# An fp32 Fourier-mixing and feed-forward kernel: moving columns read by turns from the two halves of a row, sums with the residual read in steps of four

## The chip, the cores and the metric

The kernel runs on one core of a Trainium2 chip. The metric is the device time of one execution in microseconds (us), the median of three runs; beside the runs there is one execution taken with the hardware profiler, which has its own time and the trace. The engines are called TensorE (PE, with its weight loads PEld), VectorE (DVE), ScalarE (ACT), GpSimd (POOL) and SyncE (SP).

## The reference

All arrays are fp32; S = 2048 positions, D = 512 features, F = 1792 hidden features.

```python
def reference(A_x, A_dft_seq_re, A_dft_seq_im, A_dft_hid_re, A_dft_hid_im, B_x, B_w1, B_w2):
    def _A_ref(x, dft_seq_re, dft_seq_im, dft_hid_re, dft_hid_im):
        a = jnp.einsum("bsd,ed->bse", x, dft_hid_re)
        b = jnp.einsum("bsd,ed->bse", x, dft_hid_im)
        y = jnp.einsum("ts,bse->bte", dft_seq_re, a) - jnp.einsum("ts,bse->bte", dft_seq_im, b)
        return y
    def _B_ref(x, w1, w2):
        h = jnp.einsum("bsd,df->bsf", x, w1)
        h = _silu(h)
        out = jnp.einsum("bsf,fd->bsd", h, w2)
        return out
    x = A_x
    h = x + _A_ref(_layernorm(x, axis=-1), A_dft_seq_re, A_dft_seq_im, A_dft_hid_re, A_dft_hid_im)
    h2 = h + _B_ref(_layernorm(h, axis=-1), B_w1, B_w2)
    return h2
```

So there are two residual sums: `h = x + A(...)` and `h2 = h + B(...)`.

## The kernel before

Everything is held transposed: features on the 128 partitions, positions in the free dimension, 512 positions to a row. A matmul takes a weight tile of 128x128 as the stationary operand and a row of 512 columns as the moving one, and adds into a bank of the accumulator memory with 512 fp32 columns. The columns of the moving row and of the bank stand for positions, in the same order.

To reach fp32 accuracy every operand is split into two parts, a rounded high part and the remainder (`rounded`, L263: ScalarE copies at L266, VectorE subtracts at L270 or L272). A product is then three matmuls, issued by the helper `three` (L314 to L318): high x high, high x remainder, remainder x high. In the first steps of the kernel the same three are issued in another order, grouped over four outputs (L513, L515, L517, in `plain`). The large products are done as two-by-two block products with seven instead of eight multiplications, which is why there are numbered products 1 to 7, sums of blocks before them and sums of results behind them.

The stages, in the order in which TensorE runs them:

- `plain(0, 0)`, `fast(1, 0)`: the position transform (cosine, then sine matrix) of the normalised x, for half q = 0 of the positions. Stationary: x. Moving: rows of the position matrices, from memory. Results c and m, copied out in the order in which they lie.
- `mix_fast(0)`: the feature transform. Stationary: the feature matrices. Moving: the results of the stage before. The banks are copied out by `copy_out` (L848) or added to the transposed x by `residual` (L868, by way of the `add` at L835); the sums h are stored and normalised.
- `fast(0, 1)`, `fast(1, 1)`, `mix_fast(1)`: the same for q = 1.
- `up(0)`, `down(0)`, `up(1)`, `down(1)`: the feed-forward part. `up` has the normalised h as the moving operand and puts silu of the result into tiles g. `down` has g as the moving operand. The banks of `down(0)` and the first three of `down(1)` are copied out by `keep_bank` (L1227); the last four of `down(1)` are added to h directly by `post6`, `post7`, `post5` and `post4`, where `post7` also puts a partial sum into a bank, on top of which product 4 then accumulates. The last bank leaves in two halves of 256 columns, one copied by VectorE and one by ScalarE, each with its own store (L1259 to L1266).

The order of the work on each engine is fixed by hand: every action is an event with a planned time, made from a planned matmul time (`MM_US`, 0.2265 us) and a table of shifts by event number (`MOVED`); the events are sorted by that time, and each engine issues its instructions in that order. Tiles lie in 51 pages of 4 KB per partition. Accumulator memory is eight banks, allocated in pairs (`banks`, L260). Twelve bf16 matmuls (L1357) run at the start on a constant tile.

Of the kernel before, what the change touches and what calls it, by code (L numbers as in the profile page):

```python
# [11 lines left out]
AF = mybir.ActivationFunctionType  # L12
ALU = mybir.AluOpType
# [169 lines left out]
class Plan:  # L183
# [23 lines left out]
def fnet_ffn_kernel(  # L207
# [18 lines left out]
    for plan.now, *_, f in program(stub, plan.page, stub, stub, stub, stub, x, xT, seq, hid, ffn, out):  # L226
        f()
# [20 lines left out]
def program(nc, page, keep, small, psum, dram, x, xT, seq, hid, ffn, out):  # L248
# [11 lines left out]
    def banks(name):  # L260
        return psum.tile([P, 2, 512], F32, tag="ps", name=name)
# [43 lines left out]
    def newton(v, t, a, b):  # L305
# [5 lines left out]
            nc.vector.tensor_tensor(v, v, t, op=ALU.mult)  # L311
        nc.vector.scalar_tensor_tensor(b, v, 1.5, a, op0=ALU.add, op1=ALU.mult)

    def three(acc, wh, wl, mh, ml, first, last, on=False):  # L314

        nc.tensor.matmul(acc, wh, mh, start=first, stop=False, skip_group_check=on)  # L316
        nc.tensor.matmul(acc, wh, ml, start=False, stop=False, skip_group_check=on)  # L317
        nc.tensor.matmul(acc, wl, mh, start=False, stop=last, skip_group_check=on)  # L318

    events, clock = [], [0.0]  # L320

# [116 lines left out]
    raw, part, acc, C = {}, {}, {}, {}  # L438
# [56 lines left out]
    def plain(c, q):  # L495


        def mul(jj, k, tau, tiles, parts):
            hi, lo = parts
            if not acc:  # L500
                for v in ((1, 1), (0, 0), (1, 0), (0, 1)):
                    acc[c, q, *v] = banks(f"c{c}{q}{v[0]}{v[1]}")
            for a in tiles:
                todo = []
                for i in range(2):
                    w = X[i, k, jj]
                    for m in range(2):
                        d = slice(m * P, (m + 1) * P)
                        todo.append((acc[c, q, i, tau][:, m, :], w[:, 0, a, d], w[:, 1, a, d], hi[:, a, :], lo[:, a, :]))
                first, last = jj == 0 and k == 0 and a == 0, jj == 1 and k == 1 and a == 1  # L510
                if jj == 0 and tau == 0:
                    for o, wh, _, mh, _ in todo:
                        nc.tensor.matmul(o, wh, mh, start=first, stop=False)  # L513
                    for o, wh, _, _, ml in todo:
                        nc.tensor.matmul(o, wh, ml, start=False, stop=False)  # L515
                    for o, _, wl, mh, _ in todo:
                        nc.tensor.matmul(o, wl, mh, start=False, stop=last)  # L517
                else:
                    for v in todo:
                        three(*v, first, last)  # L520
# [256 lines left out]
    H, y, h = {}, {}, {}  # L777
# [52 lines left out]
    def mix_fast(q):  # L830

        bank, kept, sums = {}, {}, {}

        def add(o, a, b, op=ALU.add):
            nc.vector.tensor_tensor(o, a, b, op=op)  # L835
# [9 lines left out]

        def copy_out(name):
            t = kept[name] = page(f"{name}{q}")
            nc.scalar.activation(t, bank[name], AF.Copy)  # L848

        def mm(n, c):  # L850
            if c == 0 and n in (1, 7):
# [13 lines left out]
            bank[2] = banks(f"y{q}2")  # L865
            nc.scalar.activation(bank[2], bank[1], AF.Copy)

        def residual(tau, e, v):  # L868
            add(h[q, tau, e], v, h[q, tau, e])

        after = {
            1: [(0, seed)],
            7: [(0, lambda: copy_out(7)), (1.5, lambda: residual(1, 1, kept.pop(7)))],
            6: [(0, lambda: copy_out(6)), (1.5, lambda: residual(0, 1, kept.pop(6)))],
            2: [(0, lambda: residual(0, 0, bank[2]))],
            5: [(0, lambda: copy_out(5)), (1.5, lambda: residual(1, 1, kept.pop(5)))],
            4: [(0, lambda: residual(0, 1, bank[4])), (0.5, lambda: store_h(q, 0))],
            3: [(0, lambda: residual(1, 0, bank[3])), (0.5, lambda: store_h(q, 1))],
        }
# [300 lines left out]
    def down(q, later):  # L1180

        mov, bank, r, kept, last = {}, {}, {}, {}, []
# [5 lines left out]
        def store(mh, tau, m=slice(0, 2), queue=nc.sync):  # L1188
            queue.dma_start(out[2 * tau + q][:, 2 * mh : 2 * mh + 2, :][:, m, :], r[mh, tau][:, m, :])
# [32 lines left out]
        def add(o, a, b):  # L1222
            nc.vector.tensor_tensor(o, a, b, op=ALU.add)

        def keep_bank(n):
            kept[n] = page(f"p{n}")
            nc.scalar.activation(kept[n], bank[n], AF.Copy)  # L1227

        def post6():
            if later:  # L1230
                return keep_bank(6)
            add(kept[1], bank[6], kept[1])
            add(r[0, 1], r[0, 1], kept[1])

        def post7():
            if later:
                return keep_bank(7)
            add(kept[1], bank[7], kept[1])
            add(r[1, 0], r[1, 0], kept[1])
            last.append(banks("f4b")[:, 1, :])  # L1240
            nc.vector.tensor_copy(last[0], r[1, 0][:, 1, :])
            add(r[1, 1], r[1, 1], kept[1])

        def post5():
            if later:
                return keep_bank(5)
            for mh in range(2):
                add(r[mh, 1], bank[5], r[mh, 1])
                store(mh, 1)

        def post4(ms):
            if later:
                return keep_bank(4)
            m = ms[0]
            if not m:
                add(r[1, 0][:, m, :], bank[4][:, m, :], r[1, 0][:, m, :])
                store(1, 0, m)
                return
            for n, queue in enumerate((nc.sync, nc.scalar)):  # L1259
                part = slice(n * TB // 2, (n + 1) * TB // 2)  # L1260
                o = r[1, 0][:, m, part]
                if n:
                    nc.scalar.activation(o, bank[4][m][:, part], AF.Copy)
                else:
                    nc.vector.tensor_copy(o, bank[4][m][:, part])
                queue.dma_start(out[q][:, 2 + m, part], o)  # L1266

        def sums_later(start):
# [125 lines left out]
```

## Time and profile before

| | us |
|---|---|
| median of 3 runs | 666.18 (665.93 to 666.64) |
| the profiled execution | 665.71 |
| its span, first to last instruction | 663.9 |
| TensorE busy | 657.9 (2892 matmuls) |
| VectorE busy | 575.6 |
| ScalarE busy | 371.7 |
| GpSimd busy | 99.4 |

The mean granted TensorE clock is 1.0. The span is the part that the profile shows; the execution's own time has 1.8 us around it. Matmul durations overlap, so the time from one matmul's start to the next one's, here called the pitch, is read from the starts in the timeline and not from the durations. Line numbers (L318) are lines of the kernel, and a line can be that of a helper that many places call.

### The profile page before, as it was taken

The numbers are of one execution on the slowest core, as the hardware profiler recorded it, in microseconds if no ns is written. First come the engines' busy times: TensorE is split into PE (matmuls) and PEld (weight loads), VectorE is DVE, ScalarE is ACT, GpSimd is POOL, SyncE is SP. The second block draws the span as 40 slices with busy tenths as digits, with TensorE's granted clock in tenths as the row PEclk, the third lists the DMA queues.
The fourth block names the chain that finished last, engine by engine and source line by source line (L and its number), as shares of the span: only waits on it lengthen the run. The fifth ranks groups of instructions, "written<-read, shape, count | busy, mean of one in ns | idle before, by whom it ended". The sixth has DMA issues, their size and how long they took to land.

```text
span 663.9 us, 8288 instructions
## 1 busy us (share of the span) xinstructions
PE 657.9 (99%) x2892; PEld 541.9 (82%) x2892; DVE 575.6 (87%) x727; ACT 371.7 (56%) x476; POOL 99.4 (15%) x131
## 2 busy tenths in 40 slices
PE   9999999999999999999999999999999999999997
PEld 5888888888888888888888888888888888888885
DVE  7999989898988999989999998988998854379974
ACT  6997456664445435365674555778543555664600
POOL 0011011112003433111121005343010000000000
PEclk9999999999999999999999999999999999999999
DMA  8982899999799586999999987668979663278803
GB/s 324 370 224 48 269 353 370 313 298 302 268 363 364 165 295 127 397 330 397 322 323 412 408 321 270 237 222 315 342 276 376 226 227 118 80 258 305 324 32 128
DMA packets 59706, 184.22 MB, mean 277 GB/s; under 512 B 6800, under 2 KB 13840, under 8 KB 59664
## 3 DMA queue, kind: packets, MB, share of 16 engines
q1 hardware_dynamic: 45024, 131.22, 54.9%
q0 software_dynamic: 14352, 52.20, 24.6%
q8 instruction: 23, 0.38, 0.3%
q10 hardware_dynamic: 288, 0.26, 0.1%
q14 instruction: 19, 0.16, 0.1%
HBM read 139.34 MB, written 44.32 MB: 277 GB/s over the span
## 4 chain that ended last, share of the span: by engine, by line
PE 98%; DMA 0%; DVE 0%; ACT 0%; issue 0%; DVEq 0%
PE m L318 11%; PE m L316 11%; PE m L317 11%; PE y L318 8%; PE y L317 8%; PE y L316 8%; PE f L318 6%; PE f L317 6%; PE f L316 6%; PE c L317 4%; PE c L316 4%; PE c L318 4%; PE vx L318 3%; PE vx L317 3%; PE vx L316 3%; PE c L517 1%
## 5 line engine op out<-in xcount | busy, mean ns | idle before, releaser
L266 ACT ACTIVATE ph<-raw 128x1024 fp32r<-128x1024 f32 x102 | 106.0, 1057 | 86.7 <-PE m L318 18.6
L270 DVE TENSOR_TENSOR pl<-raw,ph 128x1024 fp32r<-128x1024 f32 x88 | 112.1, 1289 | 8.9 <-ACT ph L266 6.8
L316 PE MATMUL m<-ph,S 128*128 128x512 f32 x192 | 74.7, 389 | 0.0
L317 PE MATMUL m<-pl,S 128*128 128x512 f32 x192 | 74.7, 389 | 0.0
L318 PE MATMUL m<-ph,S 128*128 128x512 f32 x192 | 74.7, 389 | 0.0
L316 PE MATMUL f<-gth,wf 128*128 128x512 f32 x161 | 62.6, 389 | 0.0
L317 PE MATMUL f<-gtl,wf 128*128 128x512 f32 x161 | 62.6, 389 | 0.0
L318 PE MATMUL f<-gth,wf 128*128 128x512 f32 x161 | 62.6, 389 | 0.0
L266 ACT ACTIVATE gth<-g 128x1024 fp32r<-128x1024 f32 x42 | 42.6, 1052 | 32.6 <-DVE g L1208 31.6
L270 DVE TENSOR_TENSOR gtl<-g,gth 128x1024 fp32r<-128x1024 f32 x42 | 50.3, 1218 | 7.0 <-ACT gth L266 5.7
L316 PE MATMUL m<-ph,X 128*128 128x512 f32 x144 | 56.0, 389 | 0.0
L317 PE MATMUL m<-pl,X 128*128 128x512 f32 x144 | 56.0, 389 | 0.0
L318 PE MATMUL m<-ph,X 128*128 128x512 f32 x144 | 56.0, 389 | 0.0
L1079 DVE TENSOR_TENSOR g<-vx,g 128x512 f32<-128x512 f32 x28 | 19.3, 689 | 30.5 <-PE vx L318 17.9
L714 DVE TENSOR_TENSOR raw<-raw,raw 128x1024 f32<-128x1024 f32 x36 | 43.9, 1221 | 0.5
L316 PE MATMUL y<-ph,hf 128*128 128x512 f32 x112 | 43.6, 389 | 0.0
L317 PE MATMUL y<-pl,hf 128*128 128x512 f32 x112 | 43.6, 389 | 0.0
L318 PE MATMUL y<-ph,hf 128*128 128x512 f32 x112 | 43.6, 389 | 0.0
L317 PEld LDWEIGHTS m<-pl,S 128*128 128x128 f32 x192 | 36.1, 188 | 7.5
L318 PEld LDWEIGHTS m<-ph,S 128*128 128x128 f32 x192 | 36.0, 188 | 7.5
L316 PEld LDWEIGHTS m<-ph,S 128*128 128x128 f32 x192 | 36.0, 188 | 7.4
L317 PEld LDWEIGHTS f<-gtl,wf 128*128 128x128 f32 x161 | 30.2, 188 | 6.3
(408 smaller groups left out, 1541.8 us busy)
## 6 DMA issues: line engine op xcount, KB each, us to landing
raw<-in_seq SPq DMA_DIRECT2D x84, 512.0 KB, 7.4
hf<-fd SPq DMA_DIRECT2D x28, 512.0 KB, 7.6
wf<-wd SPq DMA_DIRECT2D x28, 512.0 KB, 5.8
wf<-wd SPq DMA_DIRECT2D x28, 384.0 KB, 5.5
sf<-sd SPq DMA_DIRECT2D x18, 512.0 KB, 5.3
raw<-in_seq POOLq DMA_DIRECT2D x16, 512.0 KB, 7.1
fd<-hf POOLq DMA_DIRECT2D x14, 512.0 KB, 7.3
w<-in_ffn SPq DMA_DIRECT2D x23, 256.0 KB, 5.3
```

The source lines that it names most:

```text
L266: nc.scalar.activation(hi, src, AF.Copy, scale=sign)
L270: nc.vector.tensor_tensor(lo, src, hi, op=ALU.subtract)
L316: nc.tensor.matmul(acc, wh, mh, start=first, stop=False, skip_group_check=on)
L317: nc.tensor.matmul(acc, wh, ml, start=False, stop=False, skip_group_check=on)
L318: nc.tensor.matmul(acc, wl, mh, start=False, stop=last, skip_group_check=on)
L517: nc.tensor.matmul(o, wl, mh, start=False, stop=last)
L714: nc.vector.tensor_tensor(o, a, b, op=ALU.subtract)
L1079: nc.vector.tensor_tensor(g[q, f][:, tau, :], src, g[q, f][:, tau, :], op=ALU.add)
```

## The change

Two things are done.

All matmuls but the twelve of the warm-up go through a helper `mul_add`, which hands the moving row of 512 columns to TensorE in another order: column 0, column 256, column 1, column 257, and so on, each single column from the other half of the row than the one before. The bank is written in order, so that bank column 2t + a holds row column 256a + t.

The results of the position transform are copied out as they lie, so the moving rows of the feature transform are permuted once already, and its matmuls permute them again; the same holds for `up` and `down`. After two such stages bank column 4t + b holds the position 128b + t. Where these banks are copied out or added to the residual, the bank is therefore read in steps of four columns (`summed`), and the tile on the other side is taken in its plain order (`plainly`). In `post7` the partial sum is written to its bank in steps of four. Nothing else differs: same instructions, counts, shapes, planned times and order.

```diff
+    def turned(columns):
+        return columns.rearrange("p (a t) -> p t a", a=2)
+
+    def summed(bank):
+        if len(bank.shape) == 2:
+            return bank.rearrange("p (t b) -> p b t", b=4)
+        return bank.rearrange("p m (t b) -> p m b t", b=4)
+
+    def plainly(tile):
+        if len(tile.shape) == 2:
+            return tile.rearrange("p (b t) -> p b t", b=4)
+        return tile.rearrange("p m (b t) -> p m b t", b=4)
+
+    def mul_add(acc, w, m, **flags):
+        nc.tensor.matmul(acc, w, turned(m), **flags)
+
     def three(acc, wh, wl, mh, ml, first, last, on=False):
-        nc.tensor.matmul(acc, wh, mh, start=first, stop=False, skip_group_check=on)
-        nc.tensor.matmul(acc, wh, ml, start=False, stop=False, skip_group_check=on)
-        nc.tensor.matmul(acc, wl, mh, start=False, stop=last, skip_group_check=on)
+        mul_add(acc, wh, mh, start=first, stop=False, skip_group_check=on)
+        mul_add(acc, wh, ml, start=False, stop=False, skip_group_check=on)
+        mul_add(acc, wl, mh, start=False, stop=last, skip_group_check=on)
...
         def copy_out(name):
             t = kept[name] = page(f"{name}{q}")
-            nc.scalar.activation(t, bank[name], AF.Copy)
+            nc.scalar.activation(plainly(t), summed(bank[name]), AF.Copy)
...
-        def residual(tau, e, v):
-            add(h[q, tau, e], v, h[q, tau, e])
+        def residual(tau, e, v, bank=False):
+            o = h[q, tau, e]
+            if bank:
+                add(plainly(o), summed(v), plainly(o))
+            else:
+                add(o, v, o)
...
+        def add_bank(o, n, a):
+            nc.vector.tensor_tensor(plainly(o), summed(n), plainly(a), op=ALU.add)
+
         def keep_bank(n):
             kept[n] = page(f"p{n}")
-            nc.scalar.activation(kept[n], bank[n], AF.Copy)
+            nc.scalar.activation(plainly(kept[n]), summed(bank[n]), AF.Copy)
...
-            add(kept[1], bank[6], kept[1])
+            add_bank(kept[1], bank[6], kept[1])
...
-            nc.vector.tensor_copy(last[0], r[1, 0][:, 1, :])
+            nc.vector.tensor_copy(summed(last[0]), plainly(r[1, 0][:, 1, :]))
...
             for n, queue in enumerate((nc.sync, nc.scalar)):
                 part = slice(n * TB // 2, (n + 1) * TB // 2)
                 o = r[1, 0][:, m, part]
+                a, b = plainly(r[1, 0][:, m, :])[:, 2 * n : 2 * n + 2], summed(bank[4][m])[:, 2 * n : 2 * n + 2]
                 if n:
-                    nc.scalar.activation(o, bank[4][m][:, part], AF.Copy)
+                    nc.scalar.activation(a, b, AF.Copy)
                 else:
-                    nc.vector.tensor_copy(o, bank[4][m][:, part])
+                    nc.vector.tensor_copy(a, b)
                 queue.dma_start(out[q][:, 2 + m, part], o)
```

More of the change, by code (lines that the diff above doesn't have):

```diff
@@ L512, in mul @@
                     for o, wh, _, mh, _ in todo:
-                        nc.tensor.matmul(o, wh, mh, start=first, stop=False)
+                        mul_add(o, wh, mh, start=first, stop=False)
                     for o, wh, _, _, ml in todo:
-                        nc.tensor.matmul(o, wh, ml, start=False, stop=False)
+                        mul_add(o, wh, ml, start=False, stop=False)
                     for o, _, wl, mh, _ in todo:
-                        nc.tensor.matmul(o, wl, mh, start=False, stop=last)
+                        mul_add(o, wl, mh, start=False, stop=last)
                 else:
@@ L1237, in post7 @@
                 return keep_bank(7)
-            add(kept[1], bank[7], kept[1])
+            add_bank(kept[1], bank[7], kept[1])
             add(r[1, 0], r[1, 0], kept[1])
             last.append(banks("f4b")[:, 1, :])
-            nc.vector.tensor_copy(last[0], r[1, 0][:, 1, :])
+            nc.vector.tensor_copy(summed(last[0]), plainly(r[1, 0][:, 1, :]))
             add(r[1, 1], r[1, 1], kept[1])
@@ L1247, in post5 @@
             for mh in range(2):
-                add(r[mh, 1], bank[5], r[mh, 1])
+                add_bank(r[mh, 1], bank[5], r[mh, 1])
                 store(mh, 1)
@@ L1255, in post4 @@
             if not m:
-                add(r[1, 0][:, m, :], bank[4][:, m, :], r[1, 0][:, m, :])
+                add_bank(r[1, 0][:, m, :], bank[4][:, m, :], r[1, 0][:, m, :])
                 store(1, 0, m)
```

6 lines of the change are left out of this document (3 added, 3 removed).

## The prediction

> **What bounds the kernel now.** I read the page first, for the engines and the chain that ended last.
>
> ```profile
> span 663.9 us, 8288 instructions
> PE 657.9 (99%) x2892; PEld 541.9 (82%) x2892; DVE 575.6 (87%) x727; ACT 371.7 (56%) x476; POOL 99.4 (15%) x131
> PEclk9999999999999999999999999999999999999999
> PE 98%; DMA 0%; DVE 0%; ACT 0%; issue 0%; DVEq 0%
> ```
>
> TensorE is busy for 657.9 of 663.9 us, at nine tenths or more of the granted clock in every slice, and the chain is TensorE for 98%. A busy share says little of matmuls, which overlap; what counts is the time from one start to the next, the pitch. So the second view is the timeline, TensorE alone.
>
> ```profile
> 599.89 0.39 PE L318 MATMUL f<-gth,wf 128*128 128x512 f32 x1
> ...
> 603.97 0.39 PE L318 MATMUL f<-gth,wf 128*128 128x512 f32 x1
> 20.00:640.00 620.00, 620.00 (x2737) 1.00 0.82 283
> ```
>
> Between the first two rows lie 18 starts: 4.08 us / 18 = 226.7 ns each. The third row, one stretch of the stage view for TensorE (its length, busy time, count, clock, DMA share, GB/s), gives 620 / 2737 = 226.5 ns over 620 us (slightly low, as the count takes in those that straddle the edges). So the pitch is the same in all stages, whatever DMA and the other engines do, and there is no idle time to win. The kernel is 2892 - 12 = 2880 matmuls of 512 fp32 columns (12 are the bf16 warm-up) at 226.7 ns: 652.9 us of 663.9. Only a change of the pitch itself can move this kernel by much.
>
> Is 226.7 ns what 512 columns must cost? The warm-up has the same 128x512 shape in bf16, so I take its rows next to those of a usual line (duration min/median/max), and its start in the timeline.
>
> ```profile
> L1357 PE MATMUL idle<-warm x12: 379/634/634, 1.2 to 5.3; 128*128 128x512 bf16 x12
> L1357 PEld LDWEIGHTS <-warm x12: 98/151/151, 1.2 to 5.1; 128*128 128x128 bf16 x12
> L317 PE MATMUL m<-pl,S x192: 389/389/389, 99.2 to 351.5; 128*128 128x512 f32 x192
> L317 PEld LDWEIGHTS m<-pl,S x192: 187/188/188, 99.0 to 351.2; 128*128 128x128 f32 x192
> 2.44 2.34 PE L1357 MATMUL idle<-warm 128*128 128x512 bf16 x5
> 4.89 0.81 PE L1357 MATMUL idle<-warm 128*128 128x512 bf16 x3
> 7.03 1.09 PE L515 MATMUL c<-pl,X 128*128 128x512 f32 x4
> ```
>
> The last three bf16 matmuls cover 0.81 us: (810 - 379) / 2 = 215.5 ns pitch. The five before the array was up to speed: (2340 - 634) / 4 = 426.5 ns, twice 213.3. So a column costs 213.3 / 512 ns at speed; bf16 pays some 2 ns beyond that, fp32 13.4 ns. By pitch fp32 pays 226.7 - 215.5 = 11.2 ns more than bf16, by duration 389 - 379 = 10; the mean of both is 10.6 ns a matmul, and 2880 x 10.6 = 30.5 us in the whole kernel. That is what can be at stake on the gaining side.
>
> What is the excess? Two candidates are in the rows: the weight load, which is twice as long in fp32 (188 against 98 ns), and the reading of operands that are twice as wide. The weight load as a chain can be put aside:
>
> ```profile
> 426.60 0.19 PEld L316 LDWEIGHTS y<-T5h,wS3h 128*128 128x128 f32 x1 [0.15 <-ACT g L1076]
> 426.71 0.39 PE L316 MATMUL y<-T5h,wS3h 128*128 128x512 f32 x1
> ...
> 426.94 0.40 PE L317 MATMUL y<-T5l,wS3h 128*128 128x512 f32 x1
> 426.94 0.19 PEld L318 LDWEIGHTS y<-T5h,wS3l 128*128 128x128 f32 x1
> ```
>
> Here a load came late, and its matmul began 0.11 us after the load's start; usually, as in the last two rows, a load starts with the matmul before, 0.23 us ahead. So a matmul needs its load's first 0.11 us, and 0.12 us is spare. And the excess is not a constant of the instruction: in the row of L515 above, just after a break, four fp32 matmuls with the same operand shapes go at (1090 - 390) / 3 = 233 ns before the stream settles at 226.7. A cost that depends on how the streams fall against each other looks like two reads getting in each other's way, the moving columns and the weights that load beside them.
>
> **The change part by part.**
>
> (1) All 2880 fp32 matmuls go through `mul_add`, which reads the moving row as column 0, 256, 1, 257 and so on. Instructions, weights, output bank and column count stay; each weight load stays. The rows of before show no matmul with such a read, so the cost is bounded by the nearest rows. Gaining side: the bf16 pitch, -10.6 ns, or at most the bare columns, 226.7 - 213.3 = 13.4 ns, 38.6 us in all. Losing side: if a column that is not next to the one before costs a full read slot of its own, the pitch is that of the slow warm-up rows, 426.5 ns, +200 ns a matmul. Between lies a read that collides as often as in the unsettled row: 233 ns, +6.3 ns, +18 us. I take the bf16 pitch: the excess depends on how the streams fall (233 against 226.7), and alternating between two places spreads the moving stream's accesses, so that each place is touched at half the rate and a read that loses its turn has twice the time to recover. This is an argument, not a row; it fixes the sign less well than the size.
>
> [...]
>
> (2) The sums at the end of a stage undo the order: a bank was permuted by two stages, so it is read in steps of four columns. Counted from the code: in `mix_fast` three copies on ScalarE and three adds on VectorE for each q; in `down` ten `keep_bank` copies, and of the last sums five adds and a copy on VectorE and the two last half copies, one on each engine. That is 17 on ScalarE and 13 on VectorE, all there before, with another access pattern.
>
> ```profile
> L1227 ACT ACTIVATE p<-f 128x1024 f32<-128x1024 f32 x10 | 10.0, 1024 | 9.0 <-PE f L318 9.0
> L835 DVE TENSOR_TENSOR h<-y,h 128x1024 f32<-128x1024 f32 x6 | 7.3, 1217 | 1.6 <-DMA h<-in_xT 1.5
> L270 DVE TENSOR_TENSOR wS5l<-ws,wS5h 128x1024 fp32r<-128x1024 f32 x1 | 3.0, 3026 | 0.5 <-ACT wS5h L266 0.5
> 659.05 0.39 PE L318 MATMUL f4b<-gth,wf 128*128 128x512 f32 x1
> 659.48 0.42 DVE L1265 COPY r<-f4b 128x256 f32<-128x256 f32 x1 [1.80 <-PE f4b L318]
> 659.94 0.38 ACT L1263 ACTIVATE r<-f4b 128x256 f32<-128x256 f32 x1 [26.87 <-DVE r L1265]
> 660.35 0.35 ACTq L1266 DMA_DIRECT2D out<-r  x1
> ```
>
> No row shows a read in steps; the bounds are nothing (the same time per element) and the slowest 1024-column row, 3026 ns against 1217, a factor of 2.5. I take nothing. Were it 2.5, a copy or add of 1.0 to 1.2 us becomes 2.6 to 3.0; in `mix_fast` the bank is written again only after another product's 24 matmuls, 24 x 0.227 = 5.4 us, which covers it. Only the two halves at the end lie bare, 0.42 and 0.38 us one behind the other: at most +1.2 us there. A gain below zero I exclude, for the same elements pass.
>
> (3) If TensorE gets faster, who is next? The stage view, with length, then busy us of PE, PEld, DVE, ACT, POOL:
>
> ```profile
> 20.00:220.00 200.00, 200.00 (x885) 165.64 (x884) 183.65 (x222) 124.90 (x155) 26.83 (x37) 1.00 0.88 292
> 220.00:400.00 180.00, 180.00 (x796) 149.10 (x795) 174.66 (x199) 94.96 (x105) 38.39 (x48) 1.00 0.90 318
> 400.00:520.00 120.00, 120.00 (x531) 99.33 (x530) 109.29 (x157) 73.77 (x101) 32.31 (x39) 1.00 0.79 288
> 520.00:660.00 140.00, 139.44 (x616) 115.16 (x614) 92.48 (x106) 63.65 (x91) 1.61 (x3) 1.00 0.55 189
> ```
>
> At 216.1 ns the four stretches would take TensorE 190.7, 171.6, 114.4 and 133 us. VectorE, which prepares every moving operand, needs 183.65, 174.66, 109.29 and 92.48. In the second it becomes the bound: 174.66 - 171.6 = 3.1 us given back. In the first and third it would be 96% busy, which in a strict order of instructions does not go without waits; I add 3 us, two or three VectorE instructions of 1.2 us that come late. The least is nothing; the most is that the 500 us from 20 to 520, where VectorE is over 90% busy, do not shrink at all, 500 / 0.2267 x 10.6 ns = 23.4 us given back.
>
> Sum against the profiled execution (665.7 us, span 663.9): 665.7 - 30.5 + 3.1 + 3 = 641.3; the median of the runs is 0.5 us above that execution, so **641.8 us**. With the gaining bound and no waits: 666.2 - 38.6 + 3.1 = 630.7. With the most given back: 666.2 - 30.5 + 23.4 = 659.1.
>
> **The rivals.**
>
> *Every column pays a slot of its own (slower).* The place is the moving read of each of the 2880 matmuls; the point from which it decides is a pitch above 227.1 ns, 0.2% more. If two neighbouring columns come in one access today, the alternation has no neighbours, and the pitch goes to 426.5 ns, or with the present 13.4 ns on top, 440: 2880 x 200 to 213 ns = 576 to 614 us, 1242 to 1280 us in all, with all other engines waiting. For it: fp32 already pays more than bf16, so its reading is near its limit. [...] A milder form, the pitch of the unsettled row for good, gives 666.2 + 18 = 684 us, and with half as much again 693.
>
> *Nothing changes.* If the 13.4 ns are a fixed cost of each fp32 matmul behind the reads, the order of columns does not matter, and the run stays at 666 us, within 1.3 us (0.2%, which is about what a measurement of this kernel can tell from no change). For it: the pitch is the same to 0.1 ns in all stages. Against: the row at 233 ns. [...]
>
> *VectorE takes the place.* As in (3), at its strongest 659 us; still faster, so it belongs to the forecast's range.
>
> **How the numbers follow.** Forecast, the pitch drops towards that of bf16: 0.62, own range 631 to 660 us. Nothing changes: 0.12. Pitch a little worse, 668 to 693 us: 0.09. Every column pays: 0.17, left out of the range. So the range is 631 to 693 us, faster 0.62, same 0.12, slower 0.26.
>
> **What would show it.** In the changed profile the duration of the matmuls at L316 to L318 and of their successors should read 379 to 380 ns instead of 389, and 18 starts should take 3.89 us instead of 4.08. Idle time should appear ahead of some matmuls between 220 and 400 us, released by VectorE, with VectorE close to 100% there. The copies and adds that read banks in steps should keep 1.02 and 1.22 us. Durations near 590 ns would mean the first rival; 389 the second; between 390 and 400 the mild form. I am wrong in kind if the pitch does not fall, and wrong in size if it falls and TensorE then waits for more than 6 us.

## The result and the profile after

| | before | after |
|---|---|---|
| median of the runs, us | 666.12 (665.93 to 666.64) | 651.75 (650.85 to 652.04) |
| the profiled execution, us | 665.71 | 652.04 |
| its span, us | 663.9 | 650.3 |

The ratio is 0.978, with a 95% interval of 0.976 to 0.980. The forecast was 641.8 us, so the direction is right and the gain of 14.4 us is 10 us smaller than the 24.4 us forecast.

First the page of after: span, engines, clock, and the shares of the chain that ended last.

```profile
span 650.3 us, 8288 instructions
PE 632.2 (97%) x2892; PEld 545.0 (84%) x2892; DVE 575.2 (88%) x727; ACT 370.7 (57%) x476; POOL 99.9 (15%) x131
PEclk9999999999999999999999999999999999999999
PE 40%; DVE 2%; ACT 1%; issue 1%; ACTq 0%
```

Instructions are as many as before. TensorE's share fell from 99 to 97%, and the chain, which was TensorE for 98%, now leaves it on the way. Two things therefore have to be read: the pitch, and the waits. The pitch comes from the timeline of TensorE, start and length first:

```profile
590.94 0.38 PE L329 MATMUL f<-gth,wf 128*128 128x512 f32 x1
...
594.83 0.38 PE L329 MATMUL f<-gth,wf 128*128 128x512 f32 x1
```

Between these rows lie 18 starts, 3.89 us, as the prediction said: 216 ns each. From the starts of all matmuls the median is 216 in every stage, and in undisturbed stretches the mean is 215.83, against 226.67 before. That saves 2880 x 10.84 ns = 31.2 us. The span fell by 13.6 us. The rest, 17.6 us, was given back in breaks of TensorE's stream: the waits themselves, the slow starts behind them and one stretch at a granted clock of 0.91. The stage view of after (length, then busy us of PE, PEld, DVE, ACT, POOL, with counts) shows where:

```profile
20.00:220.00 200.00, 195.82 (x901) 169.18 (x899) 186.81 (x223) 127.76 (x159) 30.40 (x37) 1.00 0.87 298
220.00:400.00 180.00, 173.93 (x792) 150.52 (x793) 174.70 (x202) 93.23 (x104) 37.52 (x52) 0.99 0.91 318
400.00:520.00 120.00, 118.86 (x548) 102.81 (x548) 111.03 (x158) 75.63 (x103) 30.10 (x35) 1.00 0.81 290
520.00:650.00 130.00, 125.53 (x582) 109.48 (x580) 87.21 (x101) 60.10 (x87) 1.61 (x3) 1.00 0.56 200
```

Compare the count in the first bracket with the prediction's rows. From 220 to 400 us TensorE started 796 matmuls before and 792 now: in that stretch the kernel is no faster at all, and VectorE is as busy as it was, 174.70 of 180 us against 174.66. From 20 to 220 us the count rose from 885 to 901, where the pitch alone would give 929.

A break is here a distance between two starts of over 238 ns, and what it costs is its length less 216 ns; each is counted in the stretch in which it begins:

| stretch, us | breaks, us | saved by the pitch, count before x 10.84 ns | VectorE's busy share before |
|---|---|---|---|
| 6 to 20 | 0.6 | | |
| 20 to 220 | 6.0 | 9.6 | 92% |
| 220 to 400 | 9.0 | 8.6 | 97% |
| 400 to 520 | 2.0 | 5.8 | 91% |
| 520 to the end | 0.0 | 6.7 | 66% |

The breaks sum to 17.65 us, and 31.2 - 17.65 = 13.6 us is the change of the span. What ended the waits, four rows from the waits of TensorE (us in total, times, longest):

```profile
PE m L329 <- DVE pl L270: 5.1, 4, 1.5
PE y L329 <- ACT ph L266: 2.1, 1, 2.1
PE c L329 <- ACT C L582: 1.4, 1, 1.4
PE f L329 <- DVE gtl L270: 1.1, 1, 1.1
```

Mostly it is the remainder (`pl`, `gtl`), which VectorE subtracts in L270; else a copy of ScalarE. Before, TensorE had no break at all beyond 20 us; the longest distance there is 233 ns. A break costs more than its wait. In the timeline around the largest:

```profile
369.69 0.38 PE L329 MATMUL y<-ph,hf 128*128 128x512 f32 x1
372.15 0.45 PE L329 MATMUL y<-ph,hf 128*128 128x512 f32 x1 [2.08 <-ACT ph L266]
...
373.55 1.06 PE L329 MATMUL y<-ph,hf 128*128 128x512 f32 x2
...
360.00:380.00 20.00, 17.92 (x76) 15.11 (x75) 19.84 (x22) 10.60 (x12) 0.55 (x1) 0.91 1.02 399
```

The wait of 2.08 us makes 2.46 us between two starts. From 373.55 on the rows are 1.06 us for two matmuls; their starts lie 426 ns apart, seven times, and the last row, the stage view of these 20 us, has a granted clock of 0.91, against 1.00 from 20 to 220 us; the slow starts behind this wait cost 1.7 us more. Nearly all other breaks are followed by one distance of 320 ns, 0.1 us more than a usual one. The instructions that read banks in steps did not get longer; the groups of L1251 and L852 (sum, mean ns, idle before):

```profile
L1251 ACT ACTIVATE p<-f 128x1024 f32<-128x1024 f32 x10 | 10.0, 1018 | 2.8 <-PE f L329 2.7
L852 DVE TENSOR_TENSOR h<-y,h 128x1024 f32<-128x1024 f32 x6 | 7.3, 1218 | 1.1 <-DMA h<-in_xT 1.1
```

They took 1024 and 1217 ns before.

### The profile page after: what moved, and what is told of

Read it like the earlier page. It is cut to its first block, busy times and chain, and to the rows that moved or that the text cites. A ratio compares the mean times of both kernels' runs of the same rounds, so it can differ in the third digit from the quotient of the medians.

```text
span 650.3 us, 8288 instructions
## 1 busy us (share of the span) xinstructions
PE 632.2 (97%) x2892; PEld 545.0 (84%) x2892; DVE 575.2 (88%) x727; ACT 370.7 (57%) x476; POOL 99.9 (15%) x131
## 5 line engine op out<-in xcount | busy, mean ns | idle before, releaser
L270 DVE TENSOR_TENSOR pl<-raw,ph 128x1024 fp32r<-128x1024 f32 x88 | 112.4, 1293 | 7.2 <-ACT ph L266 6.6
L329 PE MATMUL m<-ph,S 128*128 128x512 f32 x384 | 116.7, 379 | 0.0
L329 PE MATMUL f<-gth,wf 128*128 128x512 f32 x322 | 98.1, 379 | 0.0
L329 PE MATMUL m<-ph,X 128*128 128x512 f32 x288 | 88.5, 379 | 0.7 <-ACT c L700 0.7
L329 PE MATMUL m<-pl,S 128*128 128x512 f32 x192 | 73.1, 381 | 1.7 <-DVE pl L270 1.5
L329 PE MATMUL y<-ph,hf 128*128 128x512 f32 x224 | 68.6, 385 | 2.1 <-ACT ph L266 2.1
L329 PEld LDWEIGHTS f<-gth,wf 128*128 128x128 f32 x322 | 60.9, 189 | 8.7 <-ACT p L1251 0.2
L329 PEld LDWEIGHTS m<-ph,X 128*128 128x128 f32 x288 | 54.4, 189 | 8.7 <-ACT c L700 1.1
L270 DVE TENSOR_TENSOR gtl<-g,gth 128x1024 fp32r<-128x1024 f32 x42 | 50.3, 1220 | 5.5 <-ACT gth L266 5.4
L329 PE MATMUL c<-ph,X 128*128 128x512 f32 x176 | 51.5, 381 | 2.5 <-ACT C L582 1.4
L329 PEld LDWEIGHTS y<-ph,hf 128*128 128x128 f32 x224 | 43.2, 193 | 9.0 <-ACT ph L266 2.8
L329 PE MATMUL y<-pl,hf 128*128 128x512 f32 x112 | 43.3, 387 | 0.5 <-DVE pl L270 0.5
L329 PEld LDWEIGHTS c<-ph,X 128*128 128x128 f32 x176 | 32.9, 189 | 8.8 <-ACT C L582 1.8
```

Source lines behind the costliest of these rows:

```text
L270: nc.vector.tensor_tensor(lo, src, hi, op=ALU.subtract)
L329: nc.tensor.matmul(acc, w, turned(m), **flags)
```

## The experiments

Two questions stood to be settled. What is the excess of the pitch: a collision with the weight loads (the theory of the prediction), a cost of each column, or a constant of each matmul? And what makes the waits that ate half the gain: VectorE's lack of time, single long instructions, the order of the instructions, or the transfers? Each run has the kernel before beside it on the same chip (665.9 to 666.1 us in all); the ratios are to that.

**1. A table of pitches.** This kernel computes nothing of the reference: blocks of 24 matmuls of constant tiles, one way of reading after the other. An extract of how the row is handed over:

```python
def halves(v, n):   # n columns from each half by turns
    return v.rearrange("p (a t c) -> p t a c", a=2, c=n)
"step4": v.rearrange("p (t a) -> p a t", a=4)
"near4": v.rearrange("p (g a t) -> p g t a", a=2, t=4)
wts[:, :c]          # fewer weight columns
```

> No part of the reference is computed: this kernel runs blocks of 24 matmuls on tiles that stay in place, one block for each way of reading, and only the pitch (start to start) inside a block is of interest. Contiguous reading should give 226.7 ns and single columns by turns from two halves 215.8. Theory A, the excess of 10.9 ns comes from the moving read meeting the weight read: it goes by the weight columns, so 64 weight columns give about 221 and 32 about 218.5 ns with contiguous reading, and with 384 moving columns the excess stays near 11 ns (173 against 162 ns). Theory B, it belongs to the moving stream alone, so many ns per column: 64 and 32 weight columns stay at 226.7, and 384 columns have an excess of 8 ns (170). Theory C, a fixed cost of contiguous reading: neither changes it. If spreading over two places is what helps, pairs and fours by turns, quarters by turns and two places 16 or 32 bytes apart also come to about 216; if it is that no two columns that follow each other are neighbours, even-then-odd columns (step 2) and every fourth column (step 4) come to 216 as well, and pairs and fours stay between. bf16 should be at 215.8 either way.

The timeline of TensorE in this run, from a window within each block (start, length, count; length less one matmul's duration, by count less one, is the pitch):

```profile
30.64 3.56 PE L59 MATMUL m_whole<-mov,wts 128*128 128x512 f32 x15
36.72 3.62 PE L59 MATMUL m_half<-mov,wts 128*128 128x512 f32 x16
69.17 7.43 PE L59 MATMUL m_step<-mov,wts 128*128 128x512 f32 x16
90.65 3.62 PE L59 MATMUL m_near<-mov,wts 128*128 128x512 f32 x16
101.31 4.07 PE L59 MATMUL w_whole<-mov,wts 128*64 128x512 f32 x17
105.67 5.34 PE L59 MATMUL w_half<-mov,wts 128*64 128x512 f32 x24
18.79 11.30 PE L59 MATMUL b_half<-bm,bw 128*128 128x512 bf16 x23
```

The first gives (3560 - 389) / 14 = 226.5 ns, the second (3620 - 379) / 15 = 216.1. Means of the distances between starts, over 18 in each block:

| fp32 row of 512 read | ns | other | ns |
|---|---|---|---|
| whole, in order | 226.7 | 64 weight columns, whole / by turns | 230.0 / 215.8 |
| two halves, singly by turns | 215.8 | 32 weight columns, whole / by turns | 231.8 / 215.8 |
| two halves, pairs by turns | 340 | 384 moving columns, whole / by turns | 173.3 / 162.5 |
| two halves, fours / eights by turns | 250 / 243 | 256 moving columns, whole / by turns | 119.9 / 111.7 |
| four quarters, singly | 283 | weights in steps of 4, whole / by turns | 234.9 / 236.7 |
| steps of 2 / of 4 | 453 / 461 | bf16, whole | 215.8 |
| two places 16 or 32 bytes apart, singly | 215.8 | bf16, two halves singly by turns | 484 |

So the pitch of the changed kernel is there without anything else running. Theory A wanted the excess to shrink with fewer weight columns; it grew, to 14.2 ns at 64 columns and 16.0 at 32 (231.8 - 215.8). Theory B wanted it to go with the number of moving columns; it is 10.8 ns at 512 and at 384. At 256 it is 8.2, but there the row by turns takes 111.7 ns, as 128 columns do in experiment 2: by turns the pitch no longer falls with the columns there, so 8.2 is no measure of the excess. What holds it at 111.7 no run shows. Theory C comes nearest: about a constant of each matmul whose fp32 row is read in order. The constant does move with the way the weights are read: 226.7 with 128 columns, 230.0 and 231.8 with 64 and 32, and 233.3 with weights in steps of 2, where the row by turns takes 215.8 in all four. So a cost that goes by the weight columns, the prediction's mechanism in the form in which it could be priced, falls. That the two reads meet in some other way is not excluded; no block without weight loads was run.

**2. More of the table**, in the same manner: runs of columns, starts within a row, places at other distances.

```python
flat[:, k : k + 512]                                       # start k columns into the row
flat.rearrange("p (g two c) -> p g two c", two=2, c=c)[:, :, n % 2, :]   # c of every 2c columns
m(n).rearrange("p (g a t) -> p g t a", a=2, t=k)           # two places k columns apart
```

> No part of the reference is computed: again blocks of 24 matmuls on tiles that stay in place, for the pitch alone. The first table put the excess of contiguous fp32 reading at 10.8 ns a matmul for 512 and for 384 columns and did not lower it with fewer weight columns. Theory C (a fixed cost of a contiguous fp32 row): 128 columns show the same excess where the weight load lets it be seen, starting 4 to 16 bytes into the row changes nothing (226.7), and rows made of runs of 256, 128 or 32 columns stay near 226.7. Theory D (each new run costs anew): two runs of 256 give about 237.5 ns, four of 128 about 259. [...]

| fp32 row read | ns | | ns |
|---|---|---|---|
| starting 1 / 2 / 3 / 4 columns in | 237 / 233 / 229 / 232 | two places 8 bytes apart | 226.7 |
| 256 / 128 of twice as many | 227 / 227 | two places 64 or 256 bytes apart | 215.8 |
| 32 / 8 / 4 of twice as many | 237 / 232 / 233 | two rows, 2 KB apart, singly | 215.8 |
| 2 of every 4 | 453 | eight places, singly | 487 |
| 128 columns, whole / by turns | 111.7 / 111.6 | bf16: pairs / fours / sixteens by turns | 271 / 226.7 / 215.8 |

Theory D falls: two or four runs of columns cost nothing more (227 ns), so the excess is not paid for each run. Theory C does not hold to the nanosecond either: rows that start 1 to 4 columns in take 229 to 237 ns, and rows in 16 to 128 runs 232 to 237. Of two places read singly by turns, those 16 or 32 bytes apart in experiment 1, 64 or 256 bytes or a row of 2 KB apart here take 215.8 ns, and those 8 bytes apart 226.7, as in order. Pairs (340 ns), fours (250) and quarters (283) by turns do not reach 216, so spreading the reads over two places is not enough by itself. Reading two columns of every four takes 453 ns, double. Why a row in order pays these 10 ns is not shown by any run; that it does is.

**3 and 4. One half of the change each.** Only the 1176 matmuls of `up` and `down` read by turns, and only the sums there in steps; or only the 1704 of the two transforms. All others as before.

```diff
-        nc.tensor.matmul(acc, w, turned(m), **flags)
+        nc.tensor.matmul(acc, w, turned(m) if turn else m, **flags)   # turn=False in the other stages
```

> Turned reading in up and down alone (1176 of 2880 matmuls), with the steps of four in the last sums; position and feature transforms as before. Theory (pitch 215.8, and what is given back is TensorE waiting for operands in the place where it is lost): 1176 x 10.8 ns = 12.7 us saved, 2.1 us given back as in the changed kernel's stretch from 400 us on, so 655.5 us. Rival (VectorE is behind from the stages before, and the waits of the feed-forward part are a debt that it inherits): the waits are gone as well, 653.4 us.

> Turned reading in the position and feature transforms alone (1704 of 2880 matmuls), feed-forward part as before. Theory (given back on the spot): 1704 x 10.8 ns = 18.4 us saved, about 15.6 us given back between 6 and 400 us as in the changed kernel, so 663.3 us. Rival (the waits there are made up for later, where TensorE at the old pitch lets VectorE catch up): no wait can be made up on TensorE, which never idles later, so it would have to show fewer waits here: below 660 us.

The first gave 655.83 us (655.45 to 655.85), ratio 0.985 (0.983 to 0.986); the second 660.41 (659.78 to 661.28), ratio 0.992 (0.990 to 0.993). Their stage views, the feed-forward alone first, then the transforms alone:

```profile
220.00:400.00 180.00, 180.00 (x796) 149.17 (x795) 174.89 (x199) 94.73 (x106) 38.90 (x48) 1.00 0.92 319
400.00:520.00 120.00, 118.85 (x548) 102.68 (x547) 111.57 (x159) 75.00 (x103) 32.29 (x39) 1.00 0.81 289
```

```profile
20.00:220.00 200.00, 195.63 (x899) 168.91 (x898) 186.38 (x222) 127.34 (x157) 30.39 (x37) 1.00 0.88 297
220.00:400.00 180.00, 173.94 (x796) 149.81 (x797) 175.49 (x202) 94.59 (x107) 38.07 (x53) 1.00 0.91 320
```

The feed-forward, with 1176 x 10.84 ns = 12.7 us saved by the pitch, brings 10.1 us. The transforms, with 18.5 us saved, bring 5.5: from 220 to 400 us they start 796 matmuls in 180 us, exactly as many as with the slow pitch. The feed-forward came out as its theory said; the transforms came out between the theory (663.3) and the rival (below 660). What is given back is given back where it was saved, and VectorE was 97% busy there before.

**5. Less work for VectorE.** The 36 block differences of the fast products are left out (the products then take undifferenced blocks, 36 subtracts of 1.22 us less).

```diff
-            elif n == 6:
-                sub(o, b11, b22)
-            else:
-                sub(o, *{5: (b12, b11), 7: (b22, b12)}[n])
```

> The changed kernel without the three differences of position-matrix blocks that VectorE forms for products 5, 7 and 6 in `fast` (36 instructions of 1.22 us, 43.9 us of VectorE's 575; the blocks go on unsubtracted, that part of the computation is left out). Theory (VectorE is the bound between 20 and 400 us): most of TensorE's 15 us of waits there go, 651.8 - 12 = about 640 us, down to 637. Rival (the waits come from the order written by hand, from ScalarE or from DMA): at least 648 us.

646.19 us (646.08 to 647.92), ratio 0.971 (0.970 to 0.973), between theory and rival. VectorE's busy time on the page fell by 43.3 us, from 575.2 to 531.9; only 5.6 us came back, and breaks of 6.5 us remained from 220 to 400. All of these come after 320 us. From 220 to 320 us, where most of the relief of that stretch fell, there is no break left; after 320 us VectorE is still full. The stage view of after for 220 to 320 us, then that of this run for the same stretch and for 20 us with three waits:

```profile
220.00:320.00 100.00, 97.03 (x447) 84.31 (x448) 96.11 (x114) 49.34 (x55) 26.19 (x31) 1.00 0.86 284
...
220.00:320.00 100.00, 100.00 (x465) 87.51 (x464) 70.78 (x93) 50.09 (x57) 22.27 (x28) 1.00 0.95 317
320.00:340.00 20.00, 17.72 (x72) 14.32 (x71) 19.93 (x24) 14.10 (x16) 5.33 (x10) 0.91 0.97 309
```

So a sum over the whole kernel says little of VectorE's load: it has to be read by stretch.

**6. One difference by other engines.** Nothing is left out: for product 7 ScalarE negates one block and a DMA of GpSimd's queue adds the other.

```diff
+            elif n == 5:
+                sub(o, b12, b11)
             else:
-                sub(o, *{5: (b12, b11), 7: (b22, b12)}[n])
+                nc.scalar.activation(o, b12, AF.Copy, scale=-1.0)
+                src = seq[c, 2 + q, 2 * jj + 1].rearrange("p (a t) -> p a t", a=2)
+                nc.gpsimd.dma_start(o, src, accum_op=ALU.add)
```

> The changed kernel, whole computation, with one of the three block differences in `fast` taken from VectorE: for product 7 ScalarE negates the block in place and a DMA from GpSimd's queue adds the other block (12 instructions of 1.22 us fewer on VectorE, 12 of 1.0 us more on ScalarE, 12 adding DMAs of 512 KB more). Theory (VectorE is late by a few us at each of the places where TensorE waits): a third of what leaving all 36 out gave, 651.8 - 2 = about 650 us. Rival (GpSimd's queue, which stands waiting for others most of the time, hands the block over late, or DMA is full between 280 and 380 us): slower than 652, up to 660.

684.19 us (682.14 to 689.63), ratio 1.026 (1.023 to 1.029): slower than before the change, and beyond the 660 of the rival. The adding DMA stands in the timeline of this run, GpSimd's queue, then ScalarE and TensorE, like this:

```profile
102.77 0.89 POOL L754 DMA_DIRECT2D raw<-in_seq  x1
113.39 1.06 ACT L266 ACTIVATE ph<-raw 128x1024 fp32r<-128x1024 f32 x1 [10.13 <-DMA raw<-in_seq]
116.96 0.80 PE L329 MATMUL m<-ph,X 128*128 128x512 f32 x1 [7.07 <-ACT ph L266]
```

It was issued at 102.77 and landed at 113.30; ScalarE waited 10.13 us for it, and TensorE 7.07 us for ScalarE. VectorE was relieved, and here a transfer took its place. Over the whole run ScalarE waits 39.7 us for such blocks; in the profile of after it was 11.1.

**7. The long subtracts.** Three subtracts of L270, at 216.8, 233.4 and 259.5 us, take 3.26 us in place of 1.22, each beside a sum over partitions on GpSimd. The timeline of after, VectorE (two subtracts, the second long), GpSimd and TensorE:

```profile
215.63 4.40 DVE L270 TENSOR_TENSOR pl<-raw,ph 128x1024 fp32r<-128x1024 f32 x2
215.88 4.06 POOL L927 PARTITION_ALL_REDUCE v<-v  x1 [14.55 <-DVE v L926]
220.08 0.48 PE L329 MATMUL m<-pl,X 128*128 128x512 f32 x1 [1.23 <-DVE pl L270]
```

In this run the sums over partitions are replaced by a constant fill (the normalisation of h is then by a constant).

```diff
-        nc.gpsimd.partition_all_reduce(t[:, 1, :], t[:, 0, :], channels=P, reduce_op=REDUCE_ADD)
+        nc.gpsimd.memset(t[:, 1, :], 4.0)
```

> The changed kernel with GpSimd's sum over the partitions (8 in all, in the normalisation of h) replaced by a fill with a constant, so that the normalisation is not computed. VectorE subtracts that run beside such a sum take 2.4 to 3.3 us instead of 1.22 in the profile, three of them between 215 and 263 us, ahead of three of TensorE's waits (220, 255, 280 us). Theory (these slow subtracts make those waits): about 4.9 us gained, 647 us. Rival (VectorE is late there in any case): under 2 us, 650 or more.

646.32 us (645.79 to 648.07), ratio 0.971 (0.969 to 0.972): 5.4 us less than after. The same two subtracts, in its timeline, and its stage view:

```profile
216.35 2.35 DVE L270 TENSOR_TENSOR pl<-raw,ph 128x1024 fp32r<-128x1024 f32 x2
...
220.00:320.00 100.00, 100.00 (x464) 87.36 (x464) 95.52 (x116) 51.70 (x58) 18.66 (x30) 1.00 0.91 305
```

The breaks at 220, 255 and 280 us are gone; with the starts behind them they had cost 4.9 us; one of 0.9 us is new, at 211. VectorE is as full there as it was, 95.52 of 100 us, and TensorE does not wait: a share of 96% does not by itself make a wait. The fill also leaves GpSimd 25.8 us less to do (74.1 in place of 99.9), and what its queue gains by that was not separated from the shorter subtracts. In the kernel before, the same pair took as long, beside the same sum, as its timeline shows:

```profile
218.86 4.40 DVE L270 TENSOR_TENSOR pl<-raw,ph 128x1024 fp32r<-128x1024 f32 x2
219.47 3.71 POOL L906 PARTITION_ALL_REDUCE v<-v  x1 [13.99 <-DVE v L905]
```

TensorE did not wait there: the slower pitch of 226.7 ns covered it. Why the subtract takes 3.26 us beside the sum is not shown by any run; without the sum the two take 2.35 us together.

**8. Both left out**, the differences of 5 and the sums of 7.

> Both left out, the 36 block differences and the sums over partitions. Theory: most of VectorE's lateness between 20 and 400 us is gone, 641 to 643 us; the waits that stay are those that VectorE does not make (a bank copied out at 52 us, the feed-forward part's 2 us). Rival (order or DMA bound): no better than the better one of the two alone by more than 1 us.

648.12 us (645.37 to 648.63), ratio 0.972 (0.970 to 0.974): no better than either alone, as the rival said. The two gains do not add, because from 220 to 320 us they are the same gain: each run by itself leaves no break there. In experiment 5 the sums are still in, but the longest subtracts beside them take 2.06 and 2.78 us, so load and long subtracts are not told apart by it. From 320 to 400 us neither run gets far: the breaks are 5.5 us in after, 6.5 in experiment 5, 4.2 in 7 and 6.4 here. The timeline of this run (its fastest execution, 645.37 us), ScalarE and VectorE, then VectorE and TensorE:

```profile
310.80 1.06 ACT L266 ACTIVATE ph<-c 128x1024 fp32r<-128x1024 f32 x1 [4.31 <-DMA c<-cd]
312.83 1.22 DVE L1176 TENSOR_TENSOR Vl<-v,Vh 128x1024 fp32r<-128x1024 f32 x1 [9.34 <-ACT Vh L1175]
...
329.72 1.82 DVE L1176 TENSOR_TENSOR Ul<-u,Uh 128x768 fp32r<-128x768 f32 x2
332.59 1.22 DVE L270 TENSOR_TENSOR pl<-raw,ph 128x1024 fp32r<-128x1024 f32 x1
333.86 0.48 PE L329 MATMUL m<-pl,X 128*128 128x512 f32 x1 [1.57 <-DVE pl L270]
```

VectorE stood idle for 9.34 us behind a remainder whose high part ScalarE had queued behind a block (`c` from `cd`) that had not landed. Twenty us later it was full again, did the sums and remainders of w2 first, as its order has it, and the remainder that TensorE needed came 1.57 us late. The time that was freed lay at another place than the one where it was short.

**9. The steps.** All matmuls by turns, the sums read as before (the positions of the result are then permuted).

```diff
-            return bank.rearrange("p (t b) -> p b t", b=4)
+            return bank.rearrange("p (b t) -> p b t", b=4)
```

> The changed kernel with every matmul turned, but the sums read their banks in plain order instead of in steps of four (the positions of the output are left in another order). Theory (reads in steps cost the same per element, and their instructions take 1.02 and 1.22 us as before): the same as the changed kernel, 651 to 652.5 us. Rival (the steps cost something that the durations do not show, on the path at the end or in the release of banks): 650.5 us or less.

650.39 us (649.45 to 651.63), ratio 0.977 (0.975 to 0.978), just inside the rival's 650.5 and overlapping with after. The medians lie 1.4 us apart, within the scatter of both; whether the steps cost something or nothing is not settled by this run, but the group of L1251 has 1017 ns here and 1018 with steps.

**10. Fewer bytes.** Only one of four blocks of the w2 sums is stored and fetched (the products with w2 use that block throughout).

```diff
-            nc.sync.dma_start(t[:, b, :], wd[p, first + n][:, b, :])
+            nc.sync.dma_start(t[:, 0:1, :], wd[p, first + n][:, 0:1, :])   # and so the stores
```

> The changed kernel with less DMA: of the prepared second feed-forward weights only one block of three or four is stored and fetched, and all products of `down` use it, so that part is not computed rightly. Between 280 and 390 us this takes some 5 MB of 40 from the DMA engines. Theory (DMA stands behind VectorE as a bound): with VectorE's work left as it is, little, 649 to 651.5 us. Rival (DMA at about 400 GB/s between 280 and 380 us is the first cause of the waits there): 646 us or less.

650.45 us (649.78 to 650.52), ratio 0.976 (0.975 to 0.978), as the theory said. The transfers of w2 are not the first cause. Other transfers stayed: from 280 to 390 us the DMA share is 0.93 here and 1.00 in after.

**11. Experiments 8 and 10 together.**

> VectorE relieved as in the run with block differences and sums over partitions left out, and DMA relieved as in the run with one weight block. In the former, VectorE sat idle for 9 us near 305 us behind a load of c that took long to land, and TensorE then waited for VectorE for 4 us between 323 and 334 us. Theory (with VectorE relieved DMA is the bound there): these waits and the one for hf at 366 us go, 640 to 643 us. Rival (it is the fixed order of the instructions, whatever the loads): as without the thinning, 645 us or more.

644.68 us (644.56 to 645.6), ratio 0.968 (0.967 to 0.970). The waits at 323 and 366 us of experiment 8 are gone, the one at 331 stays. Breaks still sum to 10 us (2.3, 5.7 and 1.7 in the three stretches): with the three suspects out, less than half of what was given back has returned, and 644.68 lies between the theory (640 to 643) and the rival (645 or more).

**12. Another order.** No instruction more or less than after: at four of TensorE's waits VectorE does the subtract that TensorE waits for first, and two block differences (2.4 us), six small steps (1.2), two remainders (1.8) and four products (2.5) behind it. The seven entries of `MOVED` that differ, gathered from their lines, are below. By the move one difference now reads a neighbour that has not been differenced yet, so that one block holds other values.

```diff
-456: -15.87,  562: 4.37, 563: 3.37,  805: 45.86, 806: 44.01,  832: 21.06, 839: -5.99
+456: -14.5,   562: 7.07, 563: 6.07,  805: 48.99, 806: 47,     832: 24.96, 839: -4.89
```

> The changed kernel with nothing left out and not one instruction added: only the order of VectorE's instructions differs, at four places where TensorE waited in the trace after the change. Behind the subtract that TensorE waited for now stand: two block differences of 1.22 us (wait that ended at 255.54 us, 1.69 us), six small steps of a norm's root, 1.15 us together (280.49, 1.53), two remainders of 0.95 us (338.75, 1.18), four products of 0.68 us (497.82, 1.24). Theory (where VectorE has slack, a wait is made by the order of its instructions and not by how many they are): three waits go and 0.4 us of the one at 280 stays, 5.2 us in all, time 646 to 648 us. Rival (VectorE is short of time there, so what was moved back makes another wait a little later, on TensorE or through ScalarE or GpSimd): the waits come again at other places, time 650 us or more. Between 648 and 650: some of the four go, and the trace has to say which.

650.81 us (649.1 to 652.28), ratio 0.977 (0.975 to 0.978): the rival holds. The waits of TensorE in this run and its stage view:

```profile
PE m L329 <- DVE pl L270: 4.1, 7, 1.2
PE y L329 <- DMA hf<-fd: 1.7, 2, 1.0
PE f L329 <- DVE gtl L270: 0.5, 1, 0.5
220.00:400.00 180.00, 174.41 (x796) 149.61 (x797) 175.72 (x202) 94.57 (x107) 38.32 (x53) 1.00 0.91 320
```

Four waits for `pl` had become seven shorter ones; the waits at 255 and 339 us are gone and others stand at 268, 274, 283 and 346. Breaks from 220 to 400 us fell from 9.0 to 7.8 us, and 796 matmuls are started there, as before the change. Two of the new waits, 1.7 us together, are for a DMA (`hf` from `fd`), and the three subtracts of 3.26 us are still in this run; so it shows that moving the work at these four places does not help, and does not tell VectorE's load from the other two.

## Why the prediction was right in kind and wrong in size

- **The pitch falls to that of bf16: right.** 215.83 ns measured; 10.84 ns a matmul in place of 10.6, 31.2 us in place of 30.5. The duration of 379 ns and the 18 starts in 3.89 us are as said. The 213.3 ns for 512 bare columns, behind the gaining bound, was the author's estimate, half of the 426.5 ns of the first bf16 matmuls; no run shows it, and the shortest pitch of 512 columns in the tables is 215.8.
- **The mechanism behind it: not borne out.** The prediction argued from the row at 233 ns that the moving reads and the weight loads collide. Experiment 1 shows the excess no smaller with a quarter of the weight columns (16.0 ns against 10.8). The row by turns takes 215.8 ns with 128, 64 and 32 weight columns, the row in order 226.7 to 231.8, and what makes that excess no run shows. The rival that nothing changes did not come true either: another order of the moving row takes the excess away. That the forecast pitch came out was in this sense luck.
- **The rival on the slower side.** A pitch a little above the 426 to 440 ns that it priced is in the tables with steps of two columns (453 ns) and of four (461), eight places (487) and bf16 by turns (484); why these are slow is not shown. For two halves read singly by turns in fp32, which is the change, the rival does not hold: 215.8. Of the ways of reading that were tried, few gain; the chance of 0.62 came from an argument that the runs do not bear out, and pairs by turns would have cost 340 ns a matmul.
- **Reading in steps costs nothing: right for the instructions**, 1018 and 1218 ns. For the whole time experiment 9 does not settle it.
- **VectorE takes the place: the step that failed, in size.** The prediction gave back 3.1 us from 220 to 400 us and 3 us elsewhere, 6.1 in all; 17.65 us were given back. It also named the point at which it would be wrong, waits of over 6 us. Two parts can be told apart. In the second stretch it set VectorE's busy time of 174.66 us against TensorE's 171.6, as if VectorE could be busy for all of it and only the sum of its work counted. Its share stayed at 97% and the whole saving of 8.6 us was lost, 9.0 us in breaks; but experiment 7 shows that the sum of its work was the wrong measure: from 220 to 320 us the breaks went with the partition sums, while VectorE's share stayed at 96%. For the first and third stretch it allowed two or three late instructions: eight breaks there end with a wait on VectorE or ScalarE, each with 0.1 us of restart, and all breaks there cost 5.95 and 2.04 us. For the restarts and for the 1.7 us at the granted clock of 0.91 it had no term. The upper bound, 23.4 us given back, was closer to what happened than the value taken. That this bound left out the time beyond 520 us, where VectorE is 66% busy, fits: nothing was lost there.
- **What makes the waits.** Leaving out the partition sums gives back 5.4 us, 4.9 of them at three breaks that follow the three subtracts of 3.26 us. Leaving out 36 differences takes away the same three breaks. From 320 to 400 us the cause is not shown: VectorE is 96 to 99% busy there in the traces of 5, 7, 8, 11 and 12, and its order, its load and the transfers are not told apart. Experiments 5 and 8 show that its mean share is not what counts: with 43 us less to do VectorE was idle for 9 us at one place in experiment 8 and full from 320 to 340 in both (19.93 of 20 us). What the remaining 10 us of experiment 11 need is open. A fresh order of all engines for the faster pitch was not tried, only four places of it.

## What to carry to other kernels

When TensorE gets faster by some per cent, list by stage the busy share of the engine that feeds it: where that was 97% in this kernel, all of the gain was lost, at 91 to 92% a third to two thirds, at 66% nothing. The share says where to look and not how much will be lost: with the partition sums out, nothing was lost from 220 to 320 us at 96%. So look next for single long instructions; one that the old pitch covered (here 3.26 us beside a partition sum) became a wait here. A change of a read pattern is worth a small table of patterns by themselves before it is built in: neighbouring choices here lie between 216 and 487 ns.

## What was not expected of the hardware

- Of the forms tried, fp32 alternation helps in one alone: singly, between two places (215.8 ns at 16 bytes apart and at each larger distance tried, 226.7 at 8). Pairs cost 340 ns, four places 283, eight 487; bf16 by turns 484.
- The first distance after most breaks is 320 ns, once; after the wait of 2.08 us seven distances of 426 ns followed, with a granted clock of 0.91 from 360 to 380 us; they and the slow starts beside them cost 1.7 us.
- Weights read in steps of four columns raise the pitch to 235 to 237 ns with either order of the moving row; a load then takes 309 to 333 ns (medians of the blocks) in place of 188, and alternation gains nothing.
- With 128 moving columns both orders take 111.7 ns, and so do 256 by turns: there the excess of a row in order no longer shows.
